# A transfer holds one batch's 16 heads and 1,024 keys: scores in 128 rows of 1,024 columns, the weighted sum in 32 matmuls

## Chip, cores and metric

The kernel runs on one core of a Trainium2 chip. The metric is the device time of one execution in microseconds; the time of a kernel is the median of its runs.

## What is computed

A decoding step of two gated branches: attention over the last 2,048 keys of a cache (8 batches, one query position, 32 query heads on 16 key heads of 128), and an MLP. The shapes are B, D = 8, 576 and F = 4,608; the cache is [8, 16, 8192, 128] for K and for V, in bfloat16.

```python
    def _A_ref(x, k_cache, v_cache, wq, wo):
        B, Sq, D = x.shape
        Hq, Dh = 32, 128
        Hkv, Sk = k_cache.shape[1], k_cache.shape[2]
        W = min(4096, max(256, Sk // 4))
        rep = Hq // Hkv
        q = (lambda x, *d: x.transpose(*d))((x @ wq).reshape(B, Sq, Hq, Dh), 0, 2, 1, 3)
        k = jnp.repeat(k_cache[:, :, Sk - W:, :], rep, axis=1)
        v = jnp.repeat(v_cache[:, :, Sk - W:, :], rep, axis=1)
        scores = jnp.einsum("bhqd,bhkd->bhqk", q, k) * (Dh ** -0.5)
        p = _softmax(scores, axis=-1)
        o = jnp.einsum("bhqk,bhkd->bhqd", p, v)
        return (lambda x, *d: x.transpose(*d))(o, 0, 2, 1, 3).reshape(B, Sq, Hq * Dh) @ wo

    def _B_ref(x, w1, b1, w2, b2):
        y = _layernorm(x, axis=-1)
        h = _gelu(jnp.einsum("bsd,df->bsf", y, w1) + b1)
        return jnp.einsum("bsf,fd->bsd", h, w2) + b2
...
    return g * a + (1 - g) * b
```

K and V together are 134.2 MB, the four weight matrices 20.1 MB.

## The kernel before

**Tiling.** K and V come in 32 transfers of 4.19 MB (`load_item`, L605 to L612), 16 of each. A transfer holds 32 pairs of batch and head (two batches) and a quarter of the keys, 512; partition p holds 128 keys of head p/4, in one run of 32 KB. There are four slots for them (`ND`, L195), taken in the order 1, 2, 0, 3 (L600 to L603). After K0, K1 and K2 the stream alternates V and K: V0, K3, V1, K4 and so on (L579 to L585), and ends with the output bias, `B_w2` and `A_wo`, in the same slots. All of these are issued on SP's queue, in this order, each once its slot is free: a K slot after its four transposes, a V slot after its weighted sum.

**A K unit** (`k_unit`, L667): for each half of the keys (rh) and of the head's dimension (hh) one VectorE transpose of 128 x 2048 words (L675) into one of two KT buffers, then a score step (L693) of 8 matmuls of 512 columns on PE, which adds into PSUM banks 0 to 3: 128 rows by 2,048 columns. A row is one query head with a part of the keys; two groups of heads' rows share a bank. Columns that do not belong to a row's head are pushed down by a mask, which is written into the banks beforehand. `softmax` (L623) takes the running maximum (L627), the exponential (L633) and then writes the mask for the next unit into the same banks (L637). `spread` (L646) transposes P (L651); in the fourth unit of a group it also merges the row parts (L657 to L664).

**A V unit** (`v_item`, L709): four copies of 32 partitions (L724, on ACT and GpSimd) lay P out into a block-diagonal buffer, which was zeroed once (L589); then 64 matmuls of 256 columns (L731) give the weighted sum in one of two banks, which VectorE adds into `O` with the rescale (L740, L742). After four units the group is scaled and masked (L745), reduced (L748), spread to two halves (L750) and added to the collected heads by a matmul (L753). At the end comes the evacuation with the gate (L756) and a transpose to `oT` (L757).

**Output.** `AccGroup` (L563) multiplies 8-column weights (`oT` or the MLP's `hT`) with 576 columns of `A_wo` or `B_w2`, as two matmuls of 288 columns, placed in two column groups of the array and adding into partitions 0 and 32 of one PSUM bank (L572). Two evacuations and two output transfers follow (L835 to L838).

**Order.** Instructions are not issued in the order of the text. A planner (`_Plan.schedule`, L62) orders each engine's by estimated costs, by priorities, and by dependences: `deps` are waited for, `after` only fixes the order of starts. The MLP's gelu (L548 to L555) runs on ACT and VectorE when the first K units are at work.

## Time and profile before

| quantity | value |
|---|---|
| median of 3 runs | 370.93 us (370.26 to 371.62) |
| the profiled execution | 371.38 us |
| its span, first to last instruction | 370.1 us |
| busy: PE, VectorE, ACT, GpSimd | 275.7, 250.5, 135.3, 78.5 us |
| moved by the DMA engines | 154.55 MB, mean 418 GB/s |
| share of the span in which SP's queue kept the 16 DMA engines at work | 97.1% |
| granted TensorE clock, mean | 0.922 |

In the profile PE is the matrix engine, PEld its weight loads, DVE is VectorE, POOL is GpSimd, SP the engine that issues most transfers. A group's line gives the line of the kernel, the engine and the operation, what is written from what with shapes, the count, the busy time, the mean ns of one, and the idle time before it with its releaser. Lines of a timeline and of the chain of waits begin with the start and the duration in us. L175 is a helper: it issues matmuls that keep the weights already loaded. The granted clock is 1.00 at full speed.

### The profile page before, as it was taken

The page shows a single profiled execution, that of the slowest core. Times are in us where ns is not written, and L with a number is a line of the kernel's source. Part 1 is how long each engine was busy: PE and PEld are TensorE (multiplying, and loading weights), DVE is VectorE, ACT ScalarE, POOL GpSimd, SP SyncE. Part 2 cuts the span into 40 slices and gives each one's busy share as a digit, 9 for nine tenths or more (in the row PEclk, how much of TensorE's full clock was granted, in tenths as well). Part 3 has the DMA queues.
Part 4 walks back from the last instruction along what each step waited for, and adds up shares of the span by engine and source line. Part 5 has one row for each costly group of instructions (what it writes and reads, how often), then busy time and mean ns, then how long its engine had stood idle before and what let it go on. Part 6 is the DMA issues. An engine that isn't in the chain of part 4 may idle for free.

```text
span 370.1 us, 3732 instructions
## 1 busy us (share of the span) xinstructions
PE 275.7 (74%) x1810; PEld 126.8 (34%) x1379; DVE 250.5 (68%) x193; ACT 135.3 (37%) x119; POOL 78.5 (21%) x78
## 2 busy tenths in 40 slices
PE   0256464569898989869788787979586869798965
PEld 0110000005271634524334341607160606167832
DVE  0722978787987979595867767677868595973200
ACT  1012106332553718261708080716252523446000
POOL 8114002100423214041404040212212130432000
PEclk9976596969999999998989998989999989999996
DMA  8999999996999999999999999999999999999993
GB/s 342 425 432 448 418 436 444 411 446 255 423 436 436 427 433 430 436 432 434 429 439 427 432 436 432 434 436 427 429 443 421 437 429 436 435 429 413 428 426 144
DMA packets 6584, 154.55 MB, mean 418 GB/s; under 512 B 764, under 2 KB 932, under 8 KB 1320
## 3 DMA queue, kind: packets, MB, share of 16 engines
q1 hardware_dynamic: 6512, 154.29, 97.1%
q8 instruction: 12, 0.20, 0.2%
q10 hardware_dynamic: 56, 0.03, 0.0%
q14 instruction: 4, 0.03, 0.0%
HBM read 154.31 MB, written 0.01 MB: 417 GB/s over the span
## 4 chain that ended last, share of the span: by engine, by line
DMA 44%; DVE 34%; PE 11%; ACT 4%; issue 4%; ACTq 0%; POOL 0%; SPq 0%
DMA arena<-in_A_k_cache_dram 36%; DVE arena L675 21%; DMA arena<-in_B_w_dram 6%; PE ps L175 5%; DVE arena L651 5%; DVE arena L627 4%; DMA arena<-in_gate_w_dram 2%; PE ps L731 2%; ACT arena L633 2%; PE ps L693 2%; ACT arena L723 1%; ACT ps L637 1%; PE ps L494 1%; PE ps L572 1%; DVE arena L555 1%
## 5 line engine op out<-in xcount | busy, mean ns | idle before, releaser
L675 DVE STREAM_TRANSPOSE arena<-arena 128x2048 f32<-128x2048 f32 x64 | 145.0, 2287 | 26.6 <-DMA arena<-in_A_k_cache_dram 24.2
L175 PE MATMUL ps<-arena 128*128 128x512 bf16 (+2 forms) x446 | 126.1, 434 | 16.5 <-DVE arena L675 14.4
L731 PE MATMUL ps<-arena 128*128 128x256 bf16 x1024 | 114.4, 273 | 2.0 <-ACT arena L723 1.8
L731 PEld LDWEIGHTS ps<-arena 128*128 128x128 bf16 x1024 | 99.9, 98 | 24.2 <-issue 10.7
L724 POOL COPY arena<-arena 32x2048 bf16<-32x2048 bf16 x30 | 56.9, 1898 | 203.0 <-PE ps L731 134.3
L633 ACT ACTIVATE arena<-ps,arena 128x2048 bf16<-128x2048 f32 x16 | 31.5, 1967 | 155.8 <-DVE arena L631 118.5
L693 PE MATMUL ps<-arena 128*128 128x512 bf16 x114 | 48.8, 428 | 49.9 <-DVE arena L675 34.3
L693 PEld LDWEIGHTS ps<-arena 128*128 128x128 bf16 x128 | 13.0, 102 | 170.6 <-DVE arena L675 99.9
L723 ACT ACTIVATE arena<-arena 32x2048 bf16<-32x2048 bf16 x32 | 61.0, 1906 | 7.3 <-PE ps L731 3.4
L627 DVE TENSOR_REDUCE arena<-ps 128x1 f32<-128x2048 f32 x16 | 36.7, 2292 | 34.8 <-PE ps L175 34.8
L651 DVE STREAM_TRANSPOSE arena<-arena 128x2048 bf16<-128x2048 bf16 x16 | 36.3, 2272 | 0.0
L637 ACT ACTIVATE ps<-arena 128x2048 f32<-128x2048 f32 x15 | 28.1, 1872 | 0.1
L572 PE MATMUL ps<-arena 128*8 128x288 bf16 (+1 forms) x140 | 12.0, 330 | 5.2 <-DMA arena<-in_A_wo_dram 4.6
L445 PE MATMUL ps<-arena 8*128 8x8 bf16 x8 | 0.6, 171 | 15.9 <-DVE arena L419 10.8
L742 DVE SCALAR_TENSOR_TENSOR arena<-arena,ps 128x256 f32<-128x256 f32 x12 | 5.4, 449 | 9.6 <-PE ps L731 9.5
L835 DVE CAST arena<-ps 8x288 bf16<-8x288 f32 x1 | 0.4, 446 | 14.1 <-PE ps L572 14.1
L572 PEld LDWEIGHTS ps<-arena 128*8 128x8 bf16 (+1 forms) x140 | 6.3, 96 | 10.6 <-DMA arena<-in_A_wo_dram 5.5
L620 POOL COPY arena<-arena 32x128 bf16<-32x128 bf16 x16 | 4.6, 287 | 21.6 <-PE ps L175 13.3
L550 DVE TENSOR_TENSOR arena<-arena 128x1152 f32<-128x1152 f32 x1 | 1.4, 1359 | 11.5 <-ACT arena L548 11.5
L750 POOL TENSOR_TENSOR arena<-arena 128x256 f32<-128x256 f32 x4 | 2.4, 612 | 28.0 <-DVE arena L748 28.0
L419 DVE COPY arena<-arena 8x64 bf16<-8x64 bf16 x2 | 0.3, 190 | 10.4 <-DMA arena<-in_gate_w_dram 10.4
L445 PEld LDWEIGHTS ps<-arena 8*128 8x128 bf16 x8 | 0.4, 112 | 16.2 <-DMA arena<-in_gate_w_dram 10.7
(101 smaller groups left out, 88.4 us busy)
## 6 DMA issues: line engine op xcount, KB each, us to landing
arena<-in_A_k_cache_dram SPq DMA_DIRECT2D x16, 4096.0 KB, 26.7
arena<-in_A_v_cache_dram SPq DMA_DIRECT2D x16, 4096.0 KB, 26.9
arena<-in_B_w_dram SPq DMA_DIRECT2D x1, 4608.0 KB, 23.3
arena<-in_A_wo_dram SPq DMA_DIRECT2D x4, 1152.0 KB, 21.6
arena<-in_A_wq_dram SPq DMA_DIRECT2D x1, 4096.0 KB, 12.8
arena<-in_B_w_dram SPq DMA_DIRECT2D x2, 1728.0 KB, 24.3
arena<-in_B_w_dram SPq DMA_DIRECT2D x1, 1152.0 KB, 22.2
arena<-in_B_w_dram SPq DMA_DIRECT2D x1, 576.0 KB, 24.3
```

The lines of the kernel that those rows point to most:

```text
L175: return e.add_instruction(mybir.InstMatmult(name=nc.get_next_instruction_name(), engine=mybir.EngineType.PE, ins=[e.lower_ap(rhs), e.lowe ...
L572: ins = e.matmul(ps[32 * j:32 * j + 8, BK_ACC, 0:JN], lhsT, rhs[:, JN * j:JN * j + JN], start=False, stop=True, skip_group_check=True, til ...
L627: mx = mx_done[n] = add("dve", lambda e: e.tensor_reduce(out=k(n, MX), in_=ps[:, 0:4, :].rearrange("p a n -> p (a n)"), axis=AXL.X, op=ALU ...
L633: ex = add("act", lambda e: e.activation(out=Pm, in_=ps[:, 0:4, :].rearrange("p a n -> p (a n)"), func=ACTF.Exp, bias=k(n, NB), scale=SCAL ...
L637: mask_done[n + 1] = add("act", lambda e: e.activation(out=ps[:, 0:4, :].rearrange("p a (n c) -> p (a n) c", c=32), in_=bass.AP(arena_f, o ...
L651: pt_done[n] = add("dve", lambda e: e.transpose(bass.AP(arena, offset=aoffs("PT") + 2048 * (n % 2), ap=[[AST, 128], [1, 2048]]), Pm), deps ...
L675: tr = add("dve", (lambda rh=rh, hh=hh, kb=kb: lambda e: e.transpose(bass.AP(arena_f, offset=foffs("KT") + kb * 2048, ap=[[AST // 2, 128], ...
L693: mm = e.matmul(*args, start=False, stop=True, skip_group_check=True) if rc == 0 else held_matmul(nc, e, *args, stop=True, skip=True)
L723: return e.activation(out=dst, in_=src, func=ACTF.Copy)
L724: return e.tensor_copy(dst, src)
L731: mm = e.matmul(ps[:, ob_, 0:256], (ktx if alt else ptx)[:, r, :], rhs, start=(r == 0), stop=(r == 63), skip_group_check=True)
L742: o_done[n] = add("dve", lambda e: e.scalar_tensor_tensor(out=Oc, in0=Oc, scalar=al, in1=ps[:, ob_, 0:256], op0=ALU.mult, op1=ALU.add), de ...
```

## The change

Item numbering: `NL` stays 16, but a unit is now one batch's 16 heads and half of the keys (1,024), so that a batch takes two units. A partition again holds 128 keys of one head, eight partitions a head. Scores of a unit fill 128 rows by 1,024 columns, in four groups of keys a row block, and two PSUM halves are used by turns. The weighted sum is 32 matmuls of 512 columns. The merge of row parts runs in three rounds (batches 0 to 3, 4 to 6, 7). L551 of the gelu (`o_w`) is ordered behind K1's fourth transpose. A weighted sum `pv` stands in the middle of the scores of the unit two further on instead of behind them. The output's two halves go to two PSUM banks from one weight load.

```diff
-        src = cache.rearrange("b h s d -> (b h) s d")[32 * g:32 * g + 32, S0 + KL * i:S0 + KL * i + KL, :].rearrange("j (x r) d -> j x (r d)", x=4)
+            b, i = divmod(n, 2)
+            src = cache[b, :, S0 + KL * i:S0 + KL * i + KL, :].rearrange("h (x r) d -> h x (r d)", x=XP)
...
+        def scores(n):
+            return ps[:, 2 * (n % 2):2 * (n % 2) + 2, :].rearrange("p a n -> p (a n)")
+
+        def mask(n, deps):
+            return add("act", lambda e: e.activation(out=scores(n).rearrange("p (n c) -> p n c", c=32), in_=bass.AP(arena_f, offset=foffs("maskv"), ap=[[AST // 2, 128], [0, 32], [1, 32]]), func=ACTF.Copy),
+                       deps=deps, name="mask%d" % n, cost=1.0, prio=4)
...
-            if n + 1 < NL:
-                mask_done[n + 1] = add("act", lambda e: e.activation(out=ps[:, 0:4, :].rearrange("p a (n c) -> p (a n) c", c=32), in_=bass.AP(arena_f, offset=foffs("maskv"), ap=[[AST // 2, 128], [0, 64], [1, 32]]), func=ACTF.Copy),
-                                       deps=[ex], name="mask%d" % (n + 1), cost=1.85, prio=4)
+            if n + 2 < NL:
+                mask_done[n + 2] = mask(n + 2, [ex])
...
-                             deps=deps, name="tr%d_%d%d" % (n, rh, hh), cost=2.3, after=tr_hist[-1:] + ([mx_done.get(n - 1)] if rh + hh == 0 else []) + ([pt_done.get(n - 1)] if rh == 1 else []))
+                             deps=deps, name="tr%d_%d%d" % (n, rh, hh), cost=2.3, after=tr_hist[-1:] + ([nb_done.get(n - 1)] if (rh, hh) == (0, 1) else []) + ([pt_done.get(n - 1)] if rh == 1 else []))
...
+                    if n and (rh, hh) == (0, 0):
+                        mx_done[n - 1].after.append(tr)
...
-                        for ee in range(2):
-                            for rc in range(4):
-                                rhs = bass.AP(arena, offset=aoffs("KT") + kb * 4096 + rc * 1024 + ee, ap=[[AST, 128], [2, 512]])
-                                args = (ps[:, rc, :], qbd[:, g % 2, 2 * hh + ee, rh, :], rhs)
+                        for gg in range(2):
+                            for ee in range(2):
+                                for rc in range(2):
+                                    rhs = bass.AP(arena, offset=aoffs("KT") + kb * 4096 + 2048 * gg + 1024 * rc + ee, ap=[[AST, 128], [2, 512]])
+                                    args = (ps[:, 2 * (n % 2) + rc, :], qbd[:, b % 2, 2 * hh + ee, 2 * rh + gg, :], rhs)
...
+            if n == 1:
+                o_w.after.append(trs[3])
...
-                for r in range(64):
-                    rhs = bass.AP(arena, offset=aoffs("RAW") + s * DE + 128 * r, ap=[[AST, 128], [SE, 2], [1, 128]])
-                    mm = e.matmul(ps[:, ob_, 0:256], (ktx if alt else ptx)[:, r, :], rhs, start=(r == 0), stop=(r == 63), skip_group_check=True)
+                for r in range(32):
+                    rhs = bass.AP(arena, offset=aoffs("RAW") + s * DE + 128 * r, ap=[[AST, 128], [4096, 4], [1, 128]])
+                    mm = e.matmul(ps[:, ob_, :], ptx[:, n % 2, r, :], rhs, start=(r == 0), stop=(r == 31), skip_group_check=True)
...
-            pv = add("pe", pv_fn, deps=deps, name="pv%d" % n, cost=7.2, after=pv_hist[-1:] + [qk_unit.get(n + 2)])
+            pv = add("pe", pv_fn, deps=deps, name="pv%d" % n, cost=7.2, after=pv_hist[-1:] + [qk_half[4 * n + (9 if n + 3 < NL else 11)] if n + 2 < NL else None])
...
+            if n + 3 < NL:
+                qk_ops[(n + 2, 1, 0)].after.append(pv)
...
-                        for j in range(NJ):
-                            ins = e.matmul(ps[32 * j:32 * j + 8, BK_ACC, 0:JN], lhsT, rhs[:, JN * j:JN * j + JN], start=False, stop=True,
-                                           skip_group_check=True, tile_position=(0, 32 * j))
+                        ins = e.matmul(ps[0:8, BK_ACC[0], 0:JN], lhsT, rhs[:, 0:JN], start=False, stop=True, skip_group_check=True, tile_position=(0, 0))
+                        if held:
+                            ins = held_matmul(nc, e, ps[0:8, BK_ACC[1], 0:JN], lhsT, rhs[:, JN:2 * JN], start=False, stop=True, skip=True, tile_size=(128, 32))
+                        else:
+                            ins = e.matmul(ps[0:8, BK_ACC[1], 0:JN], lhsT, rhs[:, JN:2 * JN], start=False, stop=True, skip_group_check=True, tile_position=(0, 0))
```

Beside these: the maximum, the exponential and the transpose of P take 1,024 columns; there are two buffers for P and two block-diagonal buffers of half the size (the second is zeroed after the gelu, whose intermediates lie in it); the reduced batches are kept side by side, each is scaled by its own merge coefficient on GpSimd and added by its own matmul (eight where there were four).

The new merge of a round, shortened:

```python
        def merge(r, after, pv_at):
            ...
            op = add("dve", lambda e: e.transpose(nbt, nbc), deps=[nb_done[2 * b1 - 1]], name="nbt%d" % r, cost=0.15, prio=3, after=after)
            ...
            wt = add("act", lambda e: e.activation(out=G(WT), in_=G(DL), func=ACTF.Exp), deps=[dl], name="wt%d" % r, cost=0.25, prio=3)
            sw = add("dve", lambda e: e.tensor_tensor(out=G(SW), in0=ssc[:, b0:b1], in1=G(WT), op=ALU.mult), deps=[wt, ss_done[b1 - 1]], name="sw%d" % r, cost=0.16, prio=3)
            su = add("pe", lambda e: e.matmul(ps[:, BK_S, 8 * r:8 * r + nb_], pair, G(SW), start=True, stop=True, skip_group_check=True), deps=[sw, o_pair, o_u], name="sum_pe%d" % r, cost=0.5, prio=3, after=[pv_at])
            ...
```

## Prediction before the result

> **What bounds the kernel now.** I read the page's slices first, then the windows around the one slice that stands out, the DMA queue's own timeline, the chain of waits, the groups, and last the timeline of the end.

> ```profile
> DMA  8999999996999999999999999999999999999993
> GB/s 342 425 432 448 418 436 444 411 446 255 423 436 436 427 433 430 436 432 434 429 439 427 432 436 432 434 436 427 429 443 421 437 429 436 435 429 413 428 426 144
> ...
> 82.00:84.00 2.00, 1.76 (x8) 0.19 (x2) 2.00 (x2) 0.00 (x0) 0.00 (x0) 1.00 0.65 279
> 84.00:86.00 2.00, 1.78 (x9) 0.10 (x1) 1.25 (x1) 0.00 (x0) 0.00 (x0) 1.00 0.04 16
> 86.00:88.00 2.00, 2.00 (x15) 0.97 (x11) 0.68 (x1) 0.00 (x0) 0.00 (x0) 1.00 0.89 262
> ```

> In the windows the columns are busy time (and instructions) of PE, PEld, DVE, ACT and POOL, then the granted clock, the DMA share and GB/s. The DMA engines are full from 2 us to 362 us but for one hole. At 432 GB/s (the windows from 100 to 340 us) six microseconds carry 2.59 MB; the three windows above carried 0.56 + 0.03 + 0.52 = 1.11 MB. So 1.48 MB, or 3.4 us, were lost there, and nothing like it is lost elsewhere: the 154.3 MB of transfers set the time, and only the hole and the two ends can give anything.

> ```profile
> 68.42 0.54 SPq L609 DMA_DIRECT2D arena<-in_A_v_cache_dram  x1
> 85.28 0.54 SPq L609 DMA_DIRECT2D arena<-in_A_k_cache_dram  x1
> ...
> 53.65 2.30 DVE arena L627
> ...
> 56.17 2.07 ACT arena L633 x2
> 58.26 1.89 ACT ps L637
> ...
> 60.28 0.59 PE ps L693
> ```

> The hole's cause: by 68.42 us the queue held 35.2 MB (10.03 MB of wq and w1, then K0, K1, K2, V0, K3, V1 of 4.19 MB each), which ran out at about 83.4. The next transfer, K4, needs K2's slot and was issued only at 85.28, its bytes coming some 1.5 us later (86.8). The slot was late because the first units go in series: scores, maximum, exponential, mask written into the same PSUM banks, next scores. The slots of K0, K1 and K2 came free at 51.6, 68.4 and 85.3, 17 us a unit, against 9.7 us for a transfer.

> ```profile
> L675 DVE STREAM_TRANSPOSE arena<-arena 128x2048 f32<-128x2048 f32 x64 | 145.0, 2287 | 26.6 <-DMA arena<-in_A_k_cache_dram 24.2
> L731 PE MATMUL ps<-arena 128*128 128x256 bf16 x1024 | 114.4, 273 | 2.0 <-ACT arena L723 1.8
> L627 DVE TENSOR_REDUCE arena<-ps 128x1 f32<-128x2048 f32 x16 | 36.7, 2292 | 34.8 <-PE ps L175 34.8
> L633 ACT ACTIVATE arena<-ps,arena 128x2048 bf16<-128x2048 f32 x16 | 31.5, 1967 | 155.8 <-DVE arena L631 118.5
> ```
> ```profile
> 342.88 7.16 PE L731 MATMUL ps<-arena 128*128 128x256 bf16 x64 [0.22 <-DMA arena<-in_A_v_cache_dram]
> 359.69 1.15 PE L572 MATMUL ps<-arena 128*8 128x288 bf16 x16 [1.60 <-DMA arena<-in_A_wo_dram]
> 365.14 3.04 PE L572 MATMUL ps<-arena 128*8 128x288 bf16 x24 [0.64 <-DMA arena<-in_B_w_dram]
> ```
> ```profile
> 279.36:282.77 3.41, 1.57 (x7) 0.10 (x1) 3.41 (x2) 0.46 (x1) 0.55 (x1) 1.00 1.00 432
> 357.87:361.28 3.41, 1.36 (x20) 0.63 (x16) 0.00 (x0) 0.00 (x0) 0.00 (x0) 1.00 0.99 420
> 361.28:364.69 3.41, 2.08 (x16) 0.86 (x16) 0.00 (x0) 0.00 (x0) 0.00 (x0) 0.50 0.77 313
> ```

> The groups give the prices. In the end, 16 output matmuls of 288 columns take 1.15 us (72 ns each, two side by side in two column groups) and the last 24 take 3.04 us, since the granted clock fell to a half at 361.3. From 23 us on its changes lie on a grid of 3.41 us (cut so in the last fence): a window with 1.57 us of PE work kept the full clock, one with 1.36 lost it.

> **The change, part by part. Transfers.** Same count, 4.19 MB each, issued in the same order on SP, a partition still takes 32 KB in one run; 16 stretches of 256 KB, 2 MiB apart, take the place of 32 of 128 KB. The trace has no such pattern. Bounds: 435 GB/s in the stage of contiguous weights (2 to 26 us) and 426 in the slowest long stage (26 to 84 us), against 432; for the 134.2 MB of K and V that is 2.1 us less to 4.4 us more. I take 0: the pattern of before, also 2 MiB from head to head, is the nearest row.

> [...]

> **Softmax.** Each unit has 1,024 columns instead of 2,048, in two PSUM halves by turns, so the mask is no longer between exponential and next scores. Halving rows: maximum 2.29 to 1.2 us (a 1,024-column PSUM copy, L509, took 1.22), transpose of P 2.27 to 1.2, exponential 1.97 to 1.0, mask 1.87 to 0.95, spreading copies 1.9 to 0.95. The K transposes stay: 4 of 2.29 us. A unit on VectorE is then 4 x 2.29 + 1.2 + 1.2 + 0.2 = 11.8 us.

> **The first units, by hand.** K0's bytes end at about 2.0 + 14.2 MB / 432 = 34.9. Its transposes no longer queue behind L551 and L552 (moved behind K1's fourth transpose), so they start at 36.3, after L550, not 39.2. At the half clock that holds there a score step takes 3.4 us (41.57 to 44.9 before) and sets K0's pace: the first two steps run from 38.6 to 42.0 and to some 44.7, and the fourth transpose, which waits for the second's buffer, ends at 47.0 (51.6 before). K1: four transposes, a maximum, a small step and a P transpose, 11.7 us: 58.7 (68.4). Then 6.6 us of moved MLP work (1.6, 1.4, 1.3, 2.3 from L551, L552, L554, L555) share VectorE with K2's 11.7: 77.0 (85.3). Bounds: 70.4 if all MLP work runs later, 82.3 if K2 still took the old 17 us on top of it. K4 must be issued by 83.4 - 1.5 = 81.9. So the hole closes, and even the worst order leaves 0.4 us of it. The next deadline is V2, behind pv0: this now stands in the middle of K2's scores, starts when they are half done at some 69 and ends at 76, against 92. K5 follows K3's transposes, about 90 against 102. The PSUM-held scores queued behind pv on PE wait for V's landing, 9.7 us after K's; the transposes need only the first half of those scores, so no K slot waits for it.

> **Steady part.** Per pair of transfers (19.4 us) VectorE has 11.8 plus about 0.75 for the sum and half of 1.7 for the batch's mask and reduction: 13.4. PE keeps its columns: 32 matmuls of 512 for 64 of 256, the same 32 score matmuls: about 14 us. ACT and GpSimd halve. New are two more weight loads in each score step (102 ns each by L693's row, so at most 0.8 us of PE a pair), a matmul like L753 for each batch instead of each pair of batches (0.7 us in 39), and the three merges: some ten VectorE steps of 0.16 us, one small ACT step and one small matmul each, behind which PE waits about 2 us at most. All is under the transfers, worth 0; its cover is 5 us a pair on PE and 6 on VectorE.

> **DMA gain.** Between 3.4 us (bytes lost in the hole) and 2.5 (the engine that ended last, after 84.0, to the new bytes at 86.5; the shares 0.88, 0.65, 0.42, 0.14 from 362 us show that some engines trail, and a landing needs all). I take 3.0.

> **End.** Output columns now go one after the other in one column group with one weight load a pair. No lone one is in the trace: by columns from L731 (7.15 us / 64 = 112 ns for 256) it is 125 ns; twice the paired 72 is 144. I take 125, since 72 holds a short burst's fill. V15 lands at 342.9 - 3.0 = 339.9; the last weighted sum, 7.0, ends at 346.9; then 4 + 48 + 64 + 24 = 140 matmuls x 0.125 = 17.5 and 0.7 for L753: PE ends at 365.1. By the data: the last big piece at 365.1 - 3.0 = 362.1, plus 24 x 0.125 = 3.0: 365.1 too. Thus PE hardly idles, every 3.41 us window has over 2.5 us of work, and the clock should stay full. The chain from sum to oT (o 0.85, mask 0.9, reduction 0.8, 0.6, 0.7, 0.5, 0.6, with hops 5.4) ends at 352.3, under 28 matmuls, L753 and 24 more (354.1), as now ordered; otherwise up to 1.5 us of hole. I add 0.4: 365.5 (368.2 before). The evacuation and output after it, 370.1 - 368.2 = 1.9, stay. At 144 ns the end would be 2.7 later.

> **Sum.** 365.5 + 1.9 = 367.4 us of span, against 370.1: 2.6 less. The profiled execution took 371.38 (370.1 and 1.3 around it); the median is 370.93, and the difference goes onto that: **368.3**.

> **Rivals.** (a) *The hole stays*, K2's slot is late by the new order: 368.3 + 3.0 = 371.3. For it: the half clock in K0. Against: 4.9 us of margin. (b) *PE is the bound of the end*, by 144 ns, a hole before oT or a clock that falls at 361.3 again (30 matmuls left, 125 more ns each: 3.8): 369.4 to 372.1, about 371. (c) *Slower: each pair of output matmuls waits for its weight load.* Price 70 loads x 96 ns (L572's row) = 6.7 us, all behind the last sum: 375.0; it decides once more than about 3.7 us of the 6.7 are open. Against: 64 loads of 98 ns and 64 matmuls of 256 columns ran in 7.15 us, 112 ns a pair. [...] (d) *The address pattern costs*: the heads' stretches get in each other's way and K and V come at 426: 372.7. For it: that rate has been seen; against: the pitch was there before. [...] (e) *It helps*, since the stretches are longer, 435: 366.2.

> **Chances.** Forecast 0.58 (its own range 367.3 to 369.3), (a) 0.10, (b) 0.12, (c) 0.06, (d) 0.08, (e) 0.06. About 0.3%, 1.1 us, is what can be told from no change: faster is below 369.8, slower above 372.0. Forecast, (e) and a third of (b): faster 0.68; (a) and the rest of (b): same 0.18; (c) and (d): slower 0.14. The range 366.4 to 372.4 leaves out (c), part of (d) and part of (e).

> **What would show it.** Right: no slice under 410 GB/s between 2 us and the end, K4 issued before 82, score units 12 us apart on VectorE at the start, the last output matmuls at about 125 ns, granted clock 1.00 there. Wrong: a hole that has moved, 250 ns for the output matmuls, idle PE before oT, or another rate in the steady part.

## The result and the profile after

| | before | after |
|---|---|---|
| median of the runs side by side | 370.99 us (4 runs) | 689.53 us (4 runs, 685.17 to 691.82) |
| ratio, 95% interval | | 1.857 (1.847 to 1.867) |
| span of the profiled execution | 370.1 us | 689.0 us |
| rate from 100 to 300 us | 432 GB/s | 213 GB/s |
| busy: PE, VectorE, ACT, GpSimd | 275.7, 250.5, 135.3, 78.5 us | 340.2, 227.6, 79.2, 59.8 us |
| granted TensorE clock, mean | 0.922 | 0.732 |

The change makes the kernel 1.86 times slower. The page of after, in part: its slices, its packets, its costliest groups and its issues of K and V:

```profile
DMA  9999999999999999999999999999999999999993
GB/s 378 327 212 213 213 213 213 212 212 213 213 212 213 212 212 217 215 213 212 226 223 213 218 215 224 217 213 217 220 213 213 213 214 222 217 211 217 203 399 137
DMA packets 6581, 154.50 MB, mean 224 GB/s; under 512 B 764, under 2 KB 932, under 8 KB 1320
...
L701 DVE STREAM_TRANSPOSE arena<-arena 128x2048 f32<-128x2048 f32 x64 | 146.6, 2295 | 340.2 <-DMA arena<-in_A_k_cache_dram 338.7
L760 PE MATMUL ps<-arena 128*128 128x512 bf16 x512 | 149.0, 463 | 173.0 <-DMA arena<-in_A_v_cache_dram 173.0
...
arena<-in_A_k_cache_dram SPq DMA_DIRECT2D x16, 4096.0 KB, 65.3
arena<-in_A_v_cache_dram SPq DMA_DIRECT2D x16, 4096.0 KB, 69.1
```

Read the first two lines together. The DMA engines are busy in every slice, more evenly than before, and yet they move half as much: 203 to 226 GB/s while K and V pass, and 378 and 399 GB/s in the first slice and the last but one, where weights do. The packets are as many and as large as before (6,581 against 6,584, 154.50 against 154.55 MB), so each takes longer: in the trace the median packet of 32 KB takes 1.213 us before and 2.531 us after. A full DMA row therefore says only that the engines always have something in hand. VectorE and PE wait 339 and 173 us for K and V; their own work is less than before on every engine but PE, and PE's 340.2 us stand at a granted clock of 0.73: the same matmuls take 270.6 us in e1 below, at 0.99. The arithmetic closes: 134.2 MB at 213 instead of 432 GB/s is 630 instead of 311 us, 319 us more, and the spans differ by 318.9.

So the question is what doubles the time of a packet. New in a transfer are its **source** (16 stretches of 256 KB, 2 MiB apart) and its **shape** (16 rows of 8 runs of 32 KB, where it was 32 rows of 4); new around it are the work and the order on the engines.

### The profile page after: what moved, and what is told of

It is laid out like the page before. It is cut to its first block, busy times and chain, and to the rows that moved or that the text cites. A ratio compares the mean times of both kernels' runs of the same rounds, so it can differ in the third digit from the quotient of the medians.

```text
span 689.0 us, 2829 instructions
## 1 busy us (share of the span) xinstructions
PE 340.2 (49%) x1313; PEld 99.4 (14%) x926; DVE 227.6 (33%) x210; ACT 79.2 (11%) x110; POOL 59.8 (9%) x97
## 2 busy tenths in 40 slices
DMA packets 6581, 154.50 MB, mean 224 GB/s; under 512 B 764, under 2 KB 932, under 8 KB 1320
## 4 chain that ended last, share of the span: by engine, by line
another core or an unknown queue 43%; PE 39%; DVE 10%; DMA 7%; issue 0%; SPq 0%; DVEq 0%
PE ps L760 22%; DVE arena L701 9%; PE ps L175 8%; PE ps L720 8%; DMA arena<-in_A_k_cache_dram 7%; PE ps L565 1%; DVE arena L634 1%; DVE arena L655 0%; PE ps L690 0%; DVE arena L543 0%; DVE arena L542 0%; DVE arena L770 0%; DVE arena L867 0%; SPq L413 0%
## 5 line engine op out<-in xcount | busy, mean ns | idle before, releaser
L701 DVE STREAM_TRANSPOSE arena<-arena 128x2048 f32<-128x2048 f32 x64 | 146.6, 2295 | 340.2 <-DMA arena<-in_A_k_cache_dram 338.7
L760 PE MATMUL ps<-arena 128*128 128x512 bf16 x512 | 149.0, 463 | 173.0 <-DMA arena<-in_A_v_cache_dram 173.0
L720 PE MATMUL ps<-arena 128*128 128x512 bf16 x256 | 119.8, 468 | 154.5 <-DVE arena L701 154.5
L175 PE MATMUL ps<-arena 128*128 128x512 bf16 (+3 forms) x387 | 144.1, 445 | 0.0
L760 PEld LDWEIGHTS ps<-arena 128*128 128x128 bf16 x512 | 57.7, 115 | 268.2 <-DMA arena<-in_A_v_cache_dram 184.7
L640 ACT ACTIVATE arena<-ps,arena 128x1024 bf16<-128x1024 f32 x16 | 17.8, 1113 | 480.0 <-DVE arena L636 256.3
L720 PEld LDWEIGHTS ps<-arena 128*128 128x128 bf16 x256 | 28.5, 111 | 275.5 <-DVE arena L701 188.6
L753 POOL COPY arena<-arena 32x1024 bf16<-32x1024 bf16 x31 | 31.9, 1030 | 362.2 <-DVE arena L655 340.8
L752 ACT ACTIVATE arena<-arena 32x1024 bf16<-32x1024 bf16 x32 | 33.7, 1052 | 35.4 <-DVE arena L655 14.1
L634 DVE TENSOR_REDUCE arena<-ps 128x1 f32<-128x1024 f32 x16 | 19.0, 1188 | 2.1 <-PE ps L175 2.1
L655 DVE STREAM_TRANSPOSE arena<-arena 128x1024 bf16<-128x1024 bf16 x16 | 19.3, 1205 | 0.2 <-ACT arena L640 0.2
L629 ACT ACTIVATE ps<-arena 128x1024 f32<-128x1024 f32 x15 | 15.3, 1021 | 0.3
L776 DVE TENSOR_REDUCE arena<-arena 128x128 f32<-128x512 f32 x8 | 8.2, 1020 | 0.3
## 6 DMA issues: line engine op xcount, KB each, us to landing
arena<-in_B_w_dram SPq DMA_DIRECT2D x1, 1152.0 KB, 34.8
```

The source lines that it names most:

```text
L175: return e.add_instruction(mybir.InstMatmult(name=nc.get_next_instruction_name(), engine=mybir.EngineType.PE, ins=[e.lower_ap(rhs), e.lowe ...
L629: return add("act", lambda e: e.activation(out=scores(n).rearrange("p (n c) -> p n c", c=32), in_=bass.AP(arena_f, offset=foffs("maskv"), ...
L634: mx = mx_done[n] = add("dve", lambda e: e.tensor_reduce(out=k(n, MX), in_=scores(n), axis=AXL.X, op=ALU.max), deps=[qk_unit[n]], name="mx ...
L640: ex = add("act", lambda e: e.activation(out=Pm[:, n % 2, :], in_=scores(n), func=ACTF.Exp, bias=final_nb(n), scale=SCALE, accum_out=k(n, S)),
L655: pt_done[n] = add("dve", lambda e: e.transpose(bass.AP(arena, offset=aoffs("PT") + 1024 * (n % 2), ap=[[AST, 128], [1, 1024]]), Pm[:, n % ...
L701: tr = add("dve", (lambda rh=rh, hh=hh, kb=kb: lambda e: e.transpose(bass.AP(arena_f, offset=foffs("KT") + kb * 2048, ap=[[AST // 2, 128], ...
```

## The experiments

All but h3 are the changed kernel or, for e2, the kernel before with other loads of K and V: f4 and g4 also take in what another queue needs, h2 and h4 put two loads ahead of them. e1 to e3, f1, f2, g1 to g3, h1 and i1 read other keys, or put them on other partitions, than the computation means. The expectations call the theories by letters: A is the pattern of addresses in the source, B the new work or order that would hold transfers back, C the 16 rows in the outermost dimension, which share the partitions out to the DMA engines in an unlucky way (the write side); D and A' are forms of A on the read side. The later ones write W for the write side and R for the reads or the count of rows. This is what came out; rates are from 100 to 300 us and packets are medians over the 32 KB ones, both of one profiled execution. The single times of f3, g4, h1, h2, h4 and i2 lie 2 to 7% apart, so their medians are rough.

| run | K and V transfer | GB/s | packet, us | median, us |
|---|---|---|---|---|
| before | 32 rows x 4 runs, 2 MiB apart | 432 | 1.213 | 371.0 |
| after | 16 x 8, 2 MiB apart | 213 | 2.531 | 689.5 |
| e1 | after's work, before's 32 x 4 | 432 | 1.213 | 366.2 |
| e2 | before's work, after's 16 x 8 | 212 | 2.532 | 686.8 |
| e3 | 16 x 8, 2.25 MiB apart | 213 | 2.532 | 689.1 |
| e4 | 16 x 8, runs 64 KB apart | 213 | 2.546 | 688.8 |
| f1 | one stretch of 4 MiB, written as 16 x 8 | 432 | 1.213 | 367.2 |
| f2 | the same, written as 32 x 4 | 433 | 1.213 | 366.5 |
| f3 | eight transfers of 16 x 1 | 219 | 2.451 | 685.2 |
| f4 | 16 x 8, GpSimd's queue | 216 | 2.480 | 713.6 |
| g1 | 16 x 8, 288 KB apart | 214 | 2.506 | 692.1 |
| g2 | 16 x 8, 4 MiB apart | 220 | 2.512 | 685.5 |
| g3 | 128 x 1, 2 MiB apart | 432 | 1.213 | 370.1 |
| g4 | f3's transfers on two queues | 242 | 2.228 | 636.4 |
| h1 | 16 x 1 onto 16 neighbouring partitions | 119 | 4.372 | 1152.6 |
| h2, h4 | after, engines shifted once | 212, 220 | 2.466, 2.382 | 696.7, 659.0 |
| i1 | 8 x 1, partitions 4 apart | 216 | 1.213 | 696.6 |
| i2 | 8 x 1, partitions 8 apart | 114, rising | 1.806 | 1065.9 |

### Work or transfer: e1 and e2

```diff
 # e1 in after; e2 puts after's line into before
-src = cache[b, :, S0 + KL * i:S0 + KL * i + KL, :].rearrange("h (x r) d -> h x (r d)", x=XP)
+g, q = divmod(n, 4)
+src = cache.rearrange("b h s d -> (b h) s d")[32 * g:32 * g + 32, S0 + 512 * q:S0 + 512 * q + 512, :].rearrange("j (x r) d -> j x (r d)", x=4)
```

> The changed kernel, whose K and V transfers read the addresses of the kernel before: 32 stretches of 128 KB (two batches, 512 keys) in place of 16 of 256 KB; partitions, sizes, slots and all engine work stay, so the scores belong to other keys than the reference's. Theory A, the address pattern halves the rate (213 for 432 GB/s): the rate is 432 again and the time about 368, as the prediction's sum had it. Theory B, the new work on the engines or its order holds the transfers back: about 690 as after. Theory C, only the count of rows in the outermost dimension (16 for 32) matters: about 368 too; this run does not tell A from C.

> The kernel before, whose K and V transfers read the addresses of the changed kernel (one batch's 16 heads, 1,024 keys, 8 partitions a head); all else as before, so its weighting belongs to other heads and keys than the reference's. Theories A and C: 134.2 MB at 213 GB/s are 630 us, 20.1 MB of weights at 430 are 47 us, with the ends some 680 to 690 us. Theory B: 371.

The two lines swap the result: 366.2 us with after's work, 686.8 with before's. The transfer alone makes the loss, and B falls. The rest of the change is even a gain: e1 against before is 0.990 (0.987 to 0.993), 4.0 us. Its slices, then the issues of K4 and V2 on SP's queue, then two windows of its end (busy time and count of PE, PEld, DVE, ACT, POOL, then the granted clock, DMA share and GB/s):

```profile
PEclk9999599999999999999999999999999999999999
DMA  8999999999999999999999999999999999999994
GB/s 347 431 438 400 459 402 459 402 459 416 442 424 435 449 411 450 416 452 411 449 420 442 424 440 431 431 442 424 447 413 449 416 446 418 449 416 420 429 429 189
```
```profile
76.50 0.54 SPq L606 DMA_DIRECT2D arena<-in_A_k_cache_dram  x1
77.08 0.60 SPq L606 DMA_DIRECT2D arena<-in_A_v_cache_dram  x1
```
```profile
82.00:88.00 6.00, 4.46 (x21) 1.40 (x15) 6.00 (x5) 4.30 (x5) 2.06 (x2) 1.00 1.00 427
...
353.00:357.00 4.00, 4.00 (x35) 1.39 (x16) 0.00 (x0) 0.00 (x0) 0.00 (x0) 1.00 1.02 431
357.00:361.00 4.00, 4.00 (x35) 1.43 (x17) 0.00 (x0) 0.00 (x0) 0.00 (x0) 1.00 0.79 322
```

Between the first slice and the last none is under 400, K4 goes out at 76.50 instead of 85.28, and PE is busy throughout the two windows of the end, with its clock at 1.00. This is the kernel that the prediction described; only its transfers are not those of the change.

### Addresses: e3, e4, g1, g2

```diff
 # e3: rows 2.25 MiB apart (g1: 288 KB, g2: 4 MiB, in the same way)
+flat = cache.rearrange("b h s d -> (b h s) d")
+src = flat[122880 * b:122880 * b + 147456, :].rearrange("(h s) d -> h s d", h=16)[:, 4096 + KL * i:4096 + KL * i + KL, :].rearrange("h (x r) d -> h x (r d)", x=XP)
 # e4: the two tiles of a batch take the runs of 128 keys by turns
+src = cache[b, :, S0:S0 + W, :].rearrange("h (x i r) d -> h x i (r d)", x=XP, i=2)[:, :, i, :]
```

> The changed kernel, whose transfers read 16 stretches of 256 KB that lie 2.25 MiB apart instead of 2 MiB (rows of the flat cache, so the data are other heads' and keys' than the reference's); the shape of the transfer, 16 x 8 x 32 KB, is the changed kernel's. Theory A with the distance of 2 MiB as its cause: rate near 432 GB/s, time 366 to 370. Theory C (the shape): about 690.

> The changed kernel with the reference's result: a unit takes every second run of 128 keys of a head's 2,048 (runs of 32 KB, 64 KB apart, for K and V alike) instead of its first or last 1,024 keys; the heads stay 2 MiB apart. If only the distance from head to head matters, with all 16 streams at the same place in their head: about 690. If streams that lie 128 KB apart within a head get in each other's way, which are now 256 KB apart: near 432 GB/s and about 368.

> The changed kernel reading 16 rows of 8 runs as it does, but with rows that begin 288 KB apart (256 KB read, 32 KB left out), so the shape can't be folded into one stretch and the rows still lie close; the data are other heads' and keys' than the reference's. Theory C (16 rows deal the partitions badly to the engines, whatever the addresses): about 689. Theory D (on the read side: 16 streams that start far apart at once, 2 or 2.25 MiB from one to the next): about 366.

> The changed kernel reading 16 rows of 8 runs that lie 4 MiB apart instead of 2 MiB (every second head of two batches, so not the reference's heads). Theory C: about 689. Theory D in the form that the distance from engine to engine decides, and that the kernel before, with two rows an engine, had 4 MiB there: about 366; in the form that far rows of 256 KB are slow whatever their distance: about 689.

Rows 288 KB, 2, 2.25 or 4 MiB apart, runs touching or 64 KB apart: always 213 to 220 GB/s. None of these distances in the source matters: 214 GB/s at 288 KB, 213 at 2 and 2.25 MiB, 220 at 4 MiB.

### Shape: f1, f2, g3

```diff
 # f1 (f2: h=32, x=4)
+flat = cache.rearrange("b h s d -> (b h s) d")
+src = flat[16384 * n:16384 * n + 16384, :].rearrange("(h x r) d -> h x (r d)", h=16, x=8)
 # g3
+src = cache.rearrange("b h s d -> (b h) s d")[:, S0 + 128 * n:S0 + 128 * n + 128, :].rearrange("j r d -> j (r d)")
```

> The changed kernel, whose K and V transfers each read one contiguous block of 4.19 MB, written as 16 rows of 8 runs of 32 KB, so the data are other heads' and keys' than the reference's. Theory C, the count of rows in the transfer's outermost source dimension decides how the partitions are dealt to the 16 DMA engines, and with 16 rows engines get in each other's way where they write: about 689, 213 GB/s. Theory A', any source addresses that lie far apart at fixed distances cost the rate: near 366, since nothing lies apart here.

> As the run with 16 x 8, but the same contiguous block is written as 32 rows of 4 runs: every partition takes the same 32 KB from the same address as there, only the shape of the source differs. Theory C: 432 GB/s and about 366. If 16 x 8 and 32 x 4 agree, the shape is not it.

> The changed kernel reading 128 rows of one run of 32 KB, one from each head of all eight batches, 2 MiB apart; not the reference's heads and keys. Theory C: 128 rows deal well, about 366. Theory D in the form that 2 MiB from row to row is what costs: about 689.

All three run at 432 or 433 GB/s. f1 is written as 16 x 8 like the changed kernel, but its source is one stretch, so that nothing holds its 16 rows apart; g3 shows that rows 2 MiB apart are no burden when there are 128 of them. In the trace the transfers of f1, f2 and g3 all name a destination of the shape [128,1], those of before and after [1,128]: f1 and f2 ended up as the same transfer of 128 rows, so that 32 x 4 is seen in before, e1 and h3 alone. What is slow is a transfer of 16 rows that can't be folded into one dimension. That is still two things: what is read in such a transfer, and which engine writes which partition.

### Smaller transfers and other queues: f3, f4, g4

```diff
 # f3; g4 puts x of 4 to 7 on ACT's queue, in the order 0, 4, 1, 5, 2, 6, 3, 7
+for x in range(XP):
+    src = cache[b, :, S0 + KL * i + 128 * x:S0 + KL * i + 128 * x + 128, :].rearrange("h r d -> h (r d)")
+    dst = bass.AP(arena, offset=x * AST + aoffs("RAW") + s * DE, ap=[[XP * AST, Hkv], [1, DE]])
 # f4
-d = dma("sp", lambda e: e.dma_start(slot(s), src), ...)
+d = dma("pool", lambda e: e.dma_start(slot(s), src), ...)
```

> The changed kernel with each K or V transfer cut into eight of 16 rows of 32 KB (run x of each of the 16 heads into partitions 8h + x), on SP in turn; addresses, partitions and the result are the changed kernel's. Theory C with the engines in step: engine e still writes partition 8e, then 8e + 1 and so on, so about 690. If it was the order in which one transfer's rows of 8 are walked, and not which partitions lie together in time: near 366 to 375.

> The changed kernel, its K and V transfers issued on GpSimd's queue instead of SP's; shapes, addresses and result are the changed kernel's. If the dealing of partitions to engines is made by the issuing queue and GpSimd's differs, the rate comes back: 366 to 375, with some waits behind the copies on GpSimd. If the source or the shape alone sets the rate, whoever issues: about 690.

> The changed kernel with the reference's result: each transfer cut into eight of 16 rows of 32 KB (run x of each head into partitions 8h + x), runs 0 to 3 on SP's queue and 4 to 7 on ACT's, so that each DMA engine has work of both halves of its eight partitions at once. If engines block each other by writing neighbouring partitions in step: the rate rises clearly over 213 GB/s, up to 432 and some 370 to 400 us with ACT's waits. If the read side sets it: about 690 as with eight transfers on one queue.

Cutting the transfer up or moving it to GpSimd's queue changes little (219 and 216 GB/s; f4's 24 us more than after's were not followed up). g4 was the first hint at the cause: the same 16-row transfers, on two queues, ran at 200 to 361 GB/s from slice to slice, 242 from 100 to 300 us; that is a rise over 219, but far from the 432 that the expectation held possible. A rate that wanders while nothing in the program changes does not belong to a fixed cost of a row; it looks like engines that hinder each other more or less, by how they happen to stand to each other.

### Which partitions: h1, i1, i2

```diff
 # h1, in f3: the 16 rows of a transfer on 16 neighbouring partitions
-dst = bass.AP(arena, offset=x * AST + ..., ap=[[XP * AST, Hkv], [1, DE]])
+dst = bass.AP(arena, offset=16 * x * AST + ..., ap=[[AST, Hkv], [1, DE]])
 # i1 and i2: transfers of 8 heads h0 to h0+7, one run x each
+dst = bass.AP(arena, offset=(8 * h0 + 32 * (x // 4) + x % 4) * AST + ..., ap=[[4 * AST, 8], [1, DE]])   # i1
+dst = bass.AP(arena, offset=(8 * h0 + x) * AST + ..., ap=[[8 * AST, 8], [1, DE]])                       # i2
```

> Each K and V tile as eight transfers of 16 rows, as in f3, but the 16 rows of a transfer go to 16 neighbouring partitions (16x to 16x+15) and not to every eighth one. This leaves each run on another partition than the computation means. Theory W (places of SBUF written in step): the 16 engines now write to half as many places at a time as in f3, so the rate is below f3's 214 to 226 GB/s, about 108 GB/s if they stay in step (about 1,300 us) and up to 210 if they drift apart. Theory R (count of rows, or reads): the reads are those of f3, so 214 to 226 GB/s and 677 to 693 us.

> Each K and V tile as sixteen transfers of 8 rows of one run each, the rows of a transfer on partitions 4 apart (8 neighbouring groups of four). This leaves most runs on another partition than the computation means. If it counts how many engines write to one place at a time (W): eight rows on eight engines, each to a place of its own, so a 32 KB packet takes 1.21 us as in the kernel before, and eight engines at 27 GB/s move 216 GB/s: about 690 us. If any transfer of few rows is slow by itself (R): packets stay at 2.4 to 2.5 us as in f3, eight engines move 107 GB/s, about 1,300 us.

> The same with the rows of a transfer 8 partitions apart, which is the layout that the computation means. W: two of the eight engines now share each place, packets take about 2.4 us, eight engines move 107 to 110 GB/s: about 1,250 to 1,330 us. R: the same as i1, whichever that is.

h1 reads exactly what f3 reads, in the same transfers, and writes it to other partitions: 119 instead of 219 GB/s, 4.37 instead of 2.45 us a packet (f3's window, then h1's):

```profile
100.00:300.00 200.00, 90.35 (x315) 26.20 (x240) 65.61 (x46) 24.55 (x31) 16.47 (x21) 0.74 1.01 219
...
100.00:300.00 200.00, 53.85 (x173) 13.53 (x120) 52.56 (x36) 19.16 (x25) 12.34 (x17) 0.62 1.00 119
```

So the write side sets the rate, and R falls for the reads. i1 and i2 have one more such pair; the slices of i1, then those of i2:

```profile
DMA  9745545545545545545545455455554554588851
GB/s 381 319 211 217 219 211 217 219 212 217 220 210 216 221 210 217 220 210 217 219 213 217 212 219 215 213 220 214 215 220 211 216 219 212 217 314 251 241 222 45
```
```profile
DMA  9455545455454555554545554545545545558650
GB/s 394 104 111 111 111 110 113 109 118 117 110 118 117 119 126 125 126 124 133 132 138 138 126 130 132 156 156 152 157 166 190 205 214 215 212 217 223 199 149 33
```

Both DMA rows stand at a half (0.50 and 0.51 from 100 to 300 us): eight rows employ 8 of the 16 engines. In i1 each of the eight moves a packet in 1.213 us, full speed; 8 x 32,768 B / 1.213 us = 216 GB/s. Few rows are not slow by themselves, so R falls altogether. In i2 the eight engines begin at half of that, 104 to 111 GB/s, and then the rate climbs through the run, with the same transfers to the same partitions, to 205 to 223 GB/s in the slices from 808 to 963 us. Two windows of i2 show it with equal DMA share and 1.9 times the rate:

```profile
100.00:200.00 100.00, 30.54 (x96) 7.34 (x64) 28.02 (x18) 10.10 (x13) 7.07 (x9) 0.62 0.50 111
...
800.00:900.00 100.00, 43.66 (x144) 11.73 (x104) 38.50 (x34) 13.97 (x20) 6.19 (x6) 0.71 0.50 209
```

Theory W would explain both: two engines that write to one place at the same moment take twice as long, and the same two are at full speed once they have drifted out of step. That is the author's inference from the rates and packet times; no trace shows a place. By W the drift is also why i2's 1,066 us lie below the 1,250 to 1,330 expected of it.

The single packets in the traces fit such a drift. They do not name their engine, but a packet can be joined to the one that begins within 0.1 us of its end, which gives an engine's packets in order. In i2, from 809 us on, three of every four packets of such a string take 1.21 to 1.22 us, and the fourth gets shorter each time: 1.67, 1.64, 1.58, 1.50, 1.38, 1.26, 1.21 us. In after itself the times repeat in fours too, but hardly move: 2.55, 2.56, 2.26, 2.55, then 2.55, 2.55, 2.18, 2.55 us. From 100 to 640 us of after a packet's time goes with that of the fourth one behind it (correlation 0.99) and not with the next one's (-0.25). The eight runs of a row go to eight neighbouring partitions, so, if an engine takes the runs of its row in order, a cycle of four would be the mark of places that are four partitions wide, and the changed kernel bears it.

### Shifting the engines once: h2 and h4, a miss

```diff
+rows = A_k_cache.rearrange("b h s d -> (b h) (s d)")
+d0 = dma("sp", lambda e: e.dma_start(slot(2)[0:124, 0:2080], rows[0:124, 0:2080]), ...)
+d1 = dma("sp", lambda e: e.dma_start(slot(2)[0:108, 8192:8192 + 7168], rows[0:108, 16384:16384 + 7168]), ...)
+slot_free = [[o_qp], [], [d0, d1], [o_hp]]     # h4: 1040 and 3584
```

> The changed kernel as it is, with two extra loads put before K0 that fill a slot before K1 overwrites it: one of 124 rows of 4,160 bytes, one of 108 rows of 14,336 bytes. [...] Theory R: the rate stays 213 GB/s and the time 685 to 705 us.

> As h2, with loads of half the size: a lag of two runs of eight. Theory W: a row of eight runs writes its first four to one place and its last four to another, so with a lag of two runs two engines share a place for half the time: between 213 and 430, about 287 GB/s, and about 500 to 560 us. Theory R: 213 GB/s and 685 to 700 us.

The steady rate stayed at 212 and 220 GB/s. But the first loads of h2 do show an effect: from 44 to 50 us, where both kernels move K alone, h2 has 302 GB/s and a median packet of 1.38 us, after 208 GB/s and 2.54 us. From 50 us on h2's packets take about 2.5 us again. The plan was a lag of four runs of 32 KB between engines that share a place, and of two in h4. Which engines the loads went to, and so what lag they made, no run shows; the loads of 4,160 and 14,336 B took 0.346 and 1.075 us each in the trace. So the loads ahead helped, as W would have it, but for some microseconds only; the author's estimates from W, 371 to 420 us in h2 and 500 to 560 in h4, which rest on that lag, were missed, and why the effect ended is not shown. The single executions (665.7 to 705.1 for h2, 636.8 and 681.3 for h4) scatter far more than before's, as do f3's and g4's.

### The gain without the loss: h3

```diff
 # in before
-stream = [("K", 0), ("K", 1), ("K", 2)]
+stream = [("K", 0), ("K", 1)]
 for vi in range(NL):
     stream.append(("V", vi))
-    if vi + 3 < NL:
-        stream.append(("K", vi + 3))
+    if vi + 2 < NL:
+        stream.append(("K", vi + 2))
...
-after=pv_hist[-1:] + [qk_unit.get(n + 2)])
+after=pv_hist[-1:] + [qk_unit.get(n + 1)])
```

> The kernel before with its own source, and its stream of transfers with K two items ahead of V instead of three (K0 K1 V0 K2 V1 K3 and so on), and each weighted sum behind the scores of the next K tile instead of the one after. If the hole at 84 us of the kernel before comes from the order in which slots come free early on, and the new order frees them sooner, the hole closes: 367 to 368 us (ratio 0.991 to 0.995). If DVE's transposes set the early releases in either order, the hole moves or stays: 370 to 373 us.

Measured 372.3 us, ratio 1.004 (1.003 to 1.006): a little slower. Its slices, and the end of its timeline on PE:

```profile
GB/s 342 424 431 450 434 413 449 438 410 450 434 411 452 434 413 450 429 418 448 431 418 448 427 426 445 424 426 448 420 431 447 420 431 447 418 434 417 411 351 2
```
```profile
342.44 9.77 PE L731 MATMUL ps<-arena 128*128 128x256 bf16 x64 [3.58 <-ACT arena L723]
352.04 0.28 PE L662 MATMUL ps<-arena 128*128 128x1 f32 x2
352.18 7.15 PE L731 MATMUL ps<-arena 128*128 128x256 bf16 x64
359.25 1.64 PE L572 MATMUL ps<-arena 128*8 128x288 bf16 x24
361.57 0.70 PE L753 MATMUL ps<-arena 128*128 128x256 f32 x2 [0.68 <-POOL arena L750]
362.20 7.03 PE L572 MATMUL ps<-arena 128*8 128x288 bf16 x112
```

The hole is gone and the last slice carries nothing: the bytes are in some 9 us before the end, in before 4. But each K now comes one item later in the stream. The last score matmuls start at 332.65 us, in before at 325.64, and the last weighted sum but one at 342.44, in before at 335.39, and at half clock (9.77 us). The last sum and 24 and 112 output matmuls stand behind it, so PE sets the end now. Neither branch of the expectation fits: the hole closed, and the time did not fall. No version that computes the same thing and beats the kernel before was found; e1, f1 and f2 are faster, but with transfers that do not put the keys where the rest of the changed kernel is laid out to find them.

## Why the prediction was wrong, point by point

**The step that failed is "Transfers": "Bounds: 435 GB/s ... and 426 ... I take 0".** It was 213, worth +319 us instead of at most 4.4. The step saw that the trace had no such pattern and then bounded it by three rates of other patterns, all of which run at the full rate. It described the change as stretches in DRAM, "2 MiB from head to head is the nearest row". A transfer has a second side, the partitions that the engines write at the same time. e1 and e2 show that the transfer alone makes the loss, h1 against f3 (119 and 219 GB/s) and i2 against i1 (114 and 216) that these partitions set the rate, and the cycle of four in after's packets ties the two together; that 32 rows are dealt to the engines in another way than 16 is inferred. No row of the trace of before bounded a transfer of 16 rows from below. So the term was not 0 give or take 4.4 us but unknown, and a range 6 us wide could not rest on it.

**Rival (d)** had the right sign and the wrong reason and price: the addresses cost nothing (213 to 220 GB/s in e3, e4, g1 and g2, as in after), and 426 GB/s was the same bound again. Rival (e), longer stretches help, falls: one stretch of 4 MiB (f1) runs at 432 as before.

**The rest held**, as e1 shows, where only the transfers are the old ones.

- *The first units*: K0, K1 and K2 free their slots at 48.6, 59.9 and 76.5, forecast 47.0, 58.7 and 77.0; K5 is issued at 90.29, forecast about 90. No hole; (a) falls. The sign "no slice under 410 GB/s" did not come true to the letter: three slices of e1 carry 400 to 402, each followed by one of 459.
- *DMA gain*: V15's sum starts at 338.06, before 342.88: 4.8 us, where 3.0 was taken. This term was too small: from 82 to 100 us e1 moved 1.61 MB more than before (427 and 430 GB/s against 186 and 416), 3.7 us at 432, as the bytes behind the hole were missed too. Where the other 1.1 us lies was not measured.
- *The end*: the output matmuls come 0.123 us apart (forecast 0.125), the clock stays at 1.00, PE ends at 363.2 (forecast 365.5; 1.8 of the 2.3 us between them are the larger DMA gain). (b) and (c) fall: the matmuls come 0.12 us apart with a weight load before them and without.
- *The sum*: 365.1 us of span against 367.4 forecast; 4.0 us gained in the medians where 2.6 were forecast.

In after itself nothing of this can pay: K4 is issued at 103.42 behind late transfers, and VectorE and PE have hundreds of idle microseconds.

## What to carry to other kernels

The price of a transfer depended here on which partitions the DMA engines write at the same time (219 and 119 GB/s with the same reads in f3 and h1), so a new count of rows is a new operation even where bytes, packets and source stay: find it in a trace or measure it alone before anything else is costed. Watch GB/s beside the DMA share, because the slow engines look as busy as those at full rate (a DMA share of 1.00 from 100 to 300 us in before and after alike); the time of one packet tells them apart (1.213 and 2.531 us). And where a change bundles a transfer with new work, swap the transfer alone, both ways: two runs split this case into a loss of some 320 us and a gain of 4.

## What the runs showed of the hardware that was not expected

- The same 16-row transfer takes 2.53 us a packet with rows 8 partitions apart and 4.37 with neighbouring ones; 8 rows 4 apart take 1.213 us on 8 engines.
- The rate can rise without any change in the program: i2 went from 104 to 223 GB/s over some 900 us, and from 809 us on every fourth packet of a string got shorter, 1.67 to 1.21 us. That engines which collide drift apart is the author's reading of it. In after the rate stayed: 203 to 226 GB/s while K and V pass.
- GpSimd's queue did not avoid it (216 GB/s), and a second queue did in part (242 GB/s from 100 to 300 us, up to 361 in a slice).
- The granted clock was lower where the same matmuls waited more: 0.73 on the mean in after, whose PE is busy 49% of the span, 0.99 in e1, busy 74%. The kernel before, with other matmuls, had 0.92 at 74%.
